# A fifth block of exponentials on VectorE in four groups of the last two quads, with a new order of all tasks

## The chip, the core and the metric

The kernel runs on one core of a Trainium2 chip. The metric is the device time of one execution in microseconds, the median of the runs. TensorE is called PE, ScalarE ACT, VectorE DVE, GpSimd POOL and SyncE SP, as in the profile.

## The reference

The input is a sequence of 2048 tokens of 640 numbers in bf16. It goes through an attention branch with 32 heads of 20 numbers each and through a mixing branch, and the two are multiplied:

```python
xn = _layernorm(x)
s = _A_ref(xn, A_wqkv, A_wo)             # softmax attention, 32 heads, then @ wo
g = _silu(_B_ref(xn, B_w1, B_w2, B_w3, B_w4))
return x + s * g

def _A_ref(x, wqkv, wo):
    ...
    scores = jnp.einsum("bhqd,bhkd->bhqk", q, k) * (Dh ** -0.5)
    p = _softmax(scores, axis=-1)
    o = jnp.einsum("bhqk,bhkd->bhqd", p, v)
    ...
def _B_ref(x, w1, w2, w3, w4):
    h = _gelu(_layernorm(x) @ w1)
    ...                                  # four column groups of h, each shifted along the sequence by 1 or 2
    x1 = x + hs @ w2
    return x1 + _gelu(_layernorm(x1) @ w3) @ w4
```

The attention needs 32 x 2048 x 2048 exponentials, 134 million.

## The kernel before

**Tiling.** The 32 heads are taken in eight quads of four (0 to 7), the 2048 queries in four chunks of 512; a quad and a chunk together are a group, written (quad, chunk). Within a group the keys come in 16 tiles of 128. For one key tile the scores of four heads fill four PSUM banks of 512 columns. Two heads (a pair of banks, 1024 columns) are computed by one step on PE: either as two matmuls over 32 rows of the array each (row form, L1596), or, where the neighbouring steps on PE are of another kind, as eight matmuls over 128 rows against queries masked by head (masked form, L1611).

**Exponentials on ACT.** `exp_act` (L1658) reads a pair of banks and writes 1024 exponentials in bf16. In a few tiles ("wide", L1640) one instruction takes all four banks. Then one set of four matmuls, one for each head, multiplies by the values and adds to bank 7 (L1409).

**Exponentials on DVE.** For some pairs of key tiles, called blocks, half of the scores go to DVE. `score_both` sends one pair of heads of a tile to ACT and the other to DVE, which multiplies the scores by a constant, adds another and writes 16-bit integers whose bits, read as bf16, are an approximate exponential (L1689). `block_bits` makes three more copies, each with a constant added to the integers (L1575 on DVE, or L1573 on POOL for those (group, block, copy) that `PP` lists), and four sets of four matmuls sum all four versions (L1587); the last two take values scaled by a constant (`VP`). Two blocks make one unit of 4096 columns; a fifth block is a unit of its own with 2048 columns. `ND` says for every group how many blocks it has, `UNITS` at which place in the row of key tiles they stand, and `BLK` which key tiles they are:

```python
self.BLK = [(2, 3), (6, 7), (10, 11), (14, 15), (0, 1)]
self.ND = ([2, 4, 4, 4],) + tuple([5, 4, 5, 4] for _ in range(6)) + ([4, 4, 4, 4],)
```

`NR` lists the places of the wide tiles (100 + place) among the tiles that are in no block. The last chunk of quad 7 is computed in two halves by other code (`last_half`).

**Repeats.** `AGAIN` names score steps, by (quad, chunk, key tile, pair), that are computed once or several times more than needed; the same result is written again.

**Ends of groups.** `normalise` transposes bank 7 (L1711, DVE), takes reciprocals, multiplies (L1724, POOL) and stores the group's result in DRAM. In quad 7 the output projection follows (L710 with 320 columns, L1823, L1842, L1885): for chunk 3 the part of the first seven quads after group (7,0), for a whole chunk after its group.

**Other work.** The B branch (w1, w2, w3, w4) and the projections for the next quads go on beside the attention, in the same queues.

**Order.** `program` makes the tasks in program order with the buffers that they read and write. A long string, `TABLE`, then gives the order of all 5722 tasks, two characters for a task and one for each PSUM bank set or buffer that it takes. `follow` decodes it, assigns the banks, and sets row or masked form by the neighbours on PE. `plan_sync` makes the semaphore waits from it. Each engine works through its own tasks in that order. A POOL task waits by semaphore for the last fast DVE task ahead of it in the table.

Of the kernel before, what the change touches and what calls it, by code (L numbers as in the profile page):

```python
# [639 lines left out]
class Gen:  # L640
# [1475 lines left out]
    r"E&p%v($C%6&q&c&d%;&r%x#',$'-$I'.%y%w$J&e$K*:#$g$h*.$%G&s$A%z$L$i'/%{%|'0&{%*;)$j$B$k&|&}&~*5#*/%'1%}#/$l'#*6&'%$'&'''(')*=$&_#5'$$m$M%~'**8#$n&:%&;%Y#*9'%J$&"
    r"<%K&=&>%T&%O'%Z%[%P%Q$o'2(K%L*>$&?(L%U*<%M%t%V%W%]%_(%`%a%b%R%^'+#0&t%X%F%H%S%I(T&#)&$%c%N&%*3'*?#&&&'&*(&+&((M*4(*@)&,&-&.&/'?%'@'A'B'C&)&L$&C#&1*0#&2&6)&M&"
    r"N&O'D&P&0&D&@&7&Q*D$*1'*E#*F#*2&E*G*R(&F*S%&G&8(*7*n#*I(&9*o'&H*M&*A'M('N*K'O*N$'P'Q*H#&A%*B*J)(N&u$&v&w'R&B*O&*C*P&'E'3(&x'4&y&z*v#*L'5'6*w('7'8*T&*X(*l#'9("
    r"*U)':*Z';'<*m#&R&I&3'=*V'>*[&*^%*](*Q*W#'F('G'H+4'I'J*Y)*_*x&+&('K*}#*y$*b&5*h'Y(*p'Z'[*k&S)'h'S#+'&'T'U']'^*s((U*~)'V'W&T'L'_*t#'X*z*{$+6#*`*q'+8(P'a$(O'`'b"
    r"'c'd*|$'e*r%'f+:$++#+,(+#*c+)'+<*e&J$*a+D#+5$*d&K+*)+F*u+W''j$'k+7'+H$+X#+Y#+Z%'l'm'n+J+9'+$#+m$'o+-+;$*j+%)'p#*g*i+M*f+(+.+n(+S+c#+e+>('q+?)+@$'r+[+G('s't+A"  # L2120
    r"&'u&m+b#+I%+g$+i+/+=+C'+d#'v$'w+E''x+f#+k$'y'z+B'|#'}+P,A+l$+0'{+U+h)+v$+p(+q&+x+o'g+V,2#,3'+T'~+r(+s%+z$+|(#($,/#+Q+O+j,-$,0$,K(,7#+N+t,.),L((%'i+K,)+~,1+L,"
    r"C$+]'.W(&#7+1(Q$,8%(',E(R+}+_#+^$+R+y$,G',I,+,*+`),4#,&+{&,5#()$(*+a,#+u',9$(+(,,6,((-,:),'+2,Q#,B$+w$(((.,$,;,T',S,,,%(/$,D#,U$&41F,l#,V%(0,F',m)(1(2,<1G(3,"
    r"H$,W,M#,N&,P$,R',X(5#,J(4(6(7,j(,Z,p#,O(8,k#(9,z$,r,d,g#(S(^(V,{&,t(,h%(:,v,n(;#(<,s$,u)(=(>,x#,y#,}((?(@,[(_((`(a(b-'#(z,e&,|,~'(c,a,^,f(-#(,Y,c-$$-+&-L-)(A"
    r"-r#-s#,i,].X(d---0,o(,`,b-%-&&,q((e-*#(W((X(Y(Z([(]-($(B-2-:&,_-,',w({(-;%-=#->)-3(H(|(}(~)#-4(D-6-B&-N(-5-<)$-C(-?#-1-9-P-@%-D(-R$(C#(E-T-Q#-/(F-A-M$#8-E$-]"
    r"(-S&-_-F-O)-7-.,=-X#-Y$-V(-a&.l(-c-8-`#.m+3,>-G.n-W(.o-b%(G-[(-w&.p-U-e-H.Y&-^'-x).Z.[.q-f-p%-{(.].^._.`#-}.a(I(J-i-q&(l.b-Z-u$.)#.c.d-t-o.f$.g-v$-~$.e.E'.h)"
    r",.i.j.*#2W(s.k)H.$%)%-y.##.F)-z$.%-|$.s-k)&$)'.''.,#)(-g.(()).-'.&.G$,?.r.6'-l-j)*.+.H%..#.8-n-h-d.1'./$.2$.I.5#.0.3(.t)+.7)(f$.M'.4.>.;-m(g(h.J$.N#(i.K$(j.u"
    r"#.v.w(k,@.x.y)3.@.O(.P'.z2Y$2b#.?.D2[.{#.<.:2h(2d$.Q2j2c).|.}2^#2e(2l(&f.A-I-J2]$.~/#2`.=2_#/$2n.L.92k#2g$.B.C2m%2i&/%#/&/'/(2}#2X(/).R.S2f2q2~$/+(/,/-/.2Z)3"
    r"&#/*3''//2r32&3*(2s33(/02t2z3,2a3)#-K(t((u3.&34(3+)(v(w30(x35#3;#37(38&(y)A3:3=%2u36)B(2o3K#39&3<&3-(3J3>)C3L#3/&2v3$#7;)D)E)F3R&2{(2w3D313k3A2p3F2y3%%)O2x3G"
    r"2|(3S)3()G.T3M(3Z#3B/13N'3#3U&)-().)/3]3W$3P(3V#3?3Q()03Y&)13X)23@3l(3m#3T3[%3C3o3n&44$3O3I3q(4v3w#3e3_3H45)3s3u&3x'3v%3E3c3a3`(m(42#3{(3^(n)V3}3p&3d3b43#3f3"
    r"r$(o3z#4#(4%4@&3y/4(p(q3|(.U.V4B%46/23~#(r4(4$#47(4')I#)J)K)L48))M4J$49#)N413g3t/3$4:'4K$):/5/64&)P#)l)Q4E#4=(4<$)R)S)T4;4.4+3h4F#4>(4?4G#4H&4A(4*4S$)U4U))4#"  # L2130
    r"4D4I4P#4C4R4O(4Q#4k$4l&)5)6)74L(4T#4V4M%)84c4i$4)4,4-4d#4f(4/4j#404g(4m);()94e#)<)=4n&4o&)>)?4X4]4Y)@4_4h)^4{#)W()X)e)Y4w&4}#4y(4x(4z4Z)Z4N)[4`4^5-#5/%4|(5&&"
    r"4W4p)]*%6-4~4[4a4b5'')_(5*#)s5)()`)a5?&5+)4q)b)c5@&5G(5,5.#5#)f#)d50595I$5$$5%#5H(5=#5<)g)h5K$5>(5J5L(4r5M)5D#)i)j5N5E%)k525()m()n5P(5V#565R&5Q#5X/9)o)p)q5S'"
    r"5A5B(5Z#5O5U&)r5])t(5C&5W))u5;5j(5Y#53515l&575T5k$5m()v)w/7585c)x5o(/85q&5[#54555:)y*&'5`5n*'*(*)**5f*+5r'){&5_5p$5y$5u'5w5{*,@g@o$)|)}@p@q@r5s)~*#5^@s@u%@v)"
    r"z5i*$@w63$@t6/#65@x@{#@i$*-61@j@k3i3j@l@|@y@z@}5b@~A#A$5h6=#6?5t$1E@m1^%1_1V#1`1W1X1Y1Z1[1a1b1k&1l1O'5g5v#1H#1m1n1c@n1o6%1I1J1K1L1M1P5a1Q1p1R1S1T6@(5}/G#/H6B"
    r"'/I6A$6.#4s/J/K60)5x(5z$6C4t4u5d5e67$69#6:(/L1e#1f1g1h1i6#6'1]5F1j5~6F68#62(6P#6Q$6$/;#/</=/>/?/@64%@h6I6&6L5|6<$6>&6(6[#/S#6^/T/U/V6;7S6d(6e#6`$6b6f#666E6R("
    r"6H6g(/W/:/X<(6Z$6o#6q6)6O6J/`#/a6S%6])6U(/b/c6V'/d6k$6s#6l&6G6T6r(/e/A#/B6u6x/C/D6t$/E6n#/F6W$6K6p%6h/M$7=/N6w6M6X#/O/P6_#7&'6D6{/Q6Y/R7</f(7?7%7@7A/g7'(6i&7"
    r"((6N6~/h/i/j/k6a$6z6c6j#6|A&6}6y70$/Y#7))/Z/[/]7*71$6m7-(7.#/^/_6v7F7+#7879<*$/x#=;/y<,7,)/z/{/|7><)(<+&6*7#<.$<4#<5'7$/}7//l#72<2(<0<3)<8$<7#/m/n/o73/p<:<6<"
    r"-(/q<<$<9#<R#</)0(#0)<>0*0+0,0-<S$<M(<K$<A<@04#<N%<?0506<Z#<]<;(07<C0809<L'<1<U$<B<=(<W&<P#<Q)<V(<J0L#7C0M0N0O0P<d$<O<f#<i#<X6+0Q<Y(0X#0Y0Z0[0]7E<D<[%<a$<F<k"
    r"<E<_#<b'0^<e(7B19#1:<T<h$1;1<1=<G7G<`(7D<j)<g<^=##<x(<m<H<z$<I1>0e#<n<y$<{%<w0f<q0g0h0i=$)<p='$7:7H=&(=(#0j<l=)0q#0r0s0t0u0v<}#<t=+$=-=*(<|<~&=,$0}#0~1#F-1$1"
    r"%1&0@'0A0B0C0D74=A$0E=@(=C=51-#1.1/1011<u12=E#=B%==(=?=_$<o<s=F#/r#=%=`$<r6,<c=G#75=/=H)A%=<(=>&<v>H/s/t76/u=1/v=.=2=3=K#/w=J$=0=M=4=67I=L'7J7M/~#=N(0#=P(7O0"  # L2140
    r"$0%0&0'=f#=I=O$7K=a(=g)0:#=Q0;0<=^0=0>0?=i#0.(=b#8V0/000102=703=j(=l=d&=c=k'=t#0F(0G0H=e(=u#0I0J0K=n&=p77=m(=o$=h=Z0R(8L0S0T0U0V0W=r#=s)=}(=w&=D13(14>#151617"
    r"18>%#=x%=8=y(=v>$$>'=T=z&>&#1'#1(1)1*=S7b>6#=|(=~)1+1,>7(={0_(0`0a8S0b0c=q=V>9&>:$>@(>A'=90d0k(0l0m1?&0n8P0o=W1@1A0p1B1C1D0w#0x=:=U>>$>*7Q>?%>4#>5&>J(0y0z0{7"
    r"P>3=R=Y>n$>o)>L=X=[>q#=]>r#>8>;$>](>B>,>->/>M#>(>_8W><&>N$>s(>+>P>O%>)>=>l#>t'>X$7L>m$>[(>^&>.>0>20|>1>R#>S(>Z>CA'>b>W$8Q7R>T(7N7T#>u>p7U7V>Y'>w#>y>d>I$7W7X7"
    r"Y>c>U)>K#>k>V>v#>z(>x&>|(>{$A.#A/A0A1>e>h8M>}A2>QA3?J#?L)?-$>`?/?#(7Z?$%7[#7]7^8N?)#?+?($7_7`?*$7a?%(>f?&#>~?A$?,#?.'>gA(#>a?[A)?2A*>j>i?F#?G(7p?B&?H(?5A+?'?"
    r"<$A,?I?=#?7?4A-?;?K#?a(?>$?8?c$A4#A5?M??%A6A7A8>D?C(AJA9?D'?b#?3?1A:(?0?U?f&?o(?O?q)?d?g(?6?:A;?E?Q?9A<?^#7i?](?_&A=?@?k&?S?`A>A??R?m#?p(?r?h#?P?N?i%>E?T7c#?"
    r"V7d@*$@+'@##>F?l(?n7e7f?~7g7h@$)?j@%$@&#?u7j$7k@.#@-'@/%7l?e@'@($@0@2'@6#7m@47n@)&7o@1$@7)@C'@3#@8#@,7q$@E7r@?$@>'?x?z@A7s@9$7t7u@:@;$@@&8T7w7x#@F8X7v?v?w@<'"
    r"8R@B(@D$@5@G7y@]#@_$?y7z@^)?s@`#?{?|@=8O?tAL(8UFnA@Fr@W#?}AC7{@H@J@K@X%@R$7|@S'@M8Y@a@Y#AAANAP(7}@L@T$@N7~ARAB#ADAE@Z(@[A_#Aa@U)AV(AW#F.A^$8##8$8)8%AZ(AT#@P>"
    r"G@V8Z80?W?X@IA`%A|$AU(AY#A]AdA~)8[8_AO(@QAQ$8&8'8(@O@b8*(8cA[&B^8+8,8-Ay&An(Ao'8.8/AbAmAK#AM%Ap(AX81(82Aq&83A{A}#Au&84Av#ASFt@cB#8586As(B/&AgB%#B1FuAt$Ar87Af"
    r"B&%AhAwAi8>?YBH(Bh$B+#8?#8@8A8B8CBJ&B-AeB.(8EBi#Ax#B0$Aj8DB4B7Az'Ac88(898:8;B'&BC(BD(AkAlB:8<8=B$B3B6BI#B()B*(B,'BKB28F(8G?ZB)FxBL&BN)BM#BE(8H8I8JBF%BOB=B@&B"
    r"n#8KBpC%(BWB58aB;BA'C&)B>&BQB`#B8C'(B?&B<8]B9BBBbBm&Bj#C($Br(Bo&BUBSBGBk%BPBRB_&8`BVBtBa(BT8e@dBd#Bq(Bs'Bc&BXC)BlC/(8d8b8^Bf8lCiC*#Be)8f(8g8h8i8j8zC1$BgC0(Bw"  # L2150
    r"BzC+#8kC;&C$8m(C3#C28n8o8p8q8rC<%C5'B}C8&C9(CE#BuBv9%8{(8|8}CGC7C,#C-$8sCD&CF&C4(8~9#C:B{B|C@#CB)C6CA(9$CCByCV&Bx@e@fB~CW'CSCMC_#C`(C=(8t(8uCJC>)C#C.8vCHCa&C"
# [81 lines left out]
```

## Time and profile before

| | |
|---|---|
| time, three runs | 795.1, 794.38, 794.72 us; median 794.72 |
| profiled execution | 794.99 us; span 793.2 us, clock 0.998 |
| ACT | busy 765.9 us, 97% of the span |
| PE | busy 773.7 us, 98% (modelled ends of matmuls) |
| DVE | busy 688.2 us, 87% |
| POOL | busy 441.5 us, 56% |
| exponentials on ACT | 726 of 1024 columns, 13 of 2048 |
| reads of scores on DVE (L1689) | 268 |

The profile is one execution. The busy time of a group of instructions counts overlapping instructions once, so that count times mean can be more than it. "Idle before" is the time that an engine stood still ahead of an instruction of the group, with what ended it behind the arrow. Windows give times from the start of the span.

### The profile page before, as it was taken

How to read it: one execution, taken by the hardware profiler on the slowest of the kernel's cores; microseconds unless marked ns; L12 is line 12 of the kernel's file. 1: busy time of each engine (PE TensorE's matmuls, PEld its weight loads, DVE VectorE, ACT ScalarE, POOL GpSimd, SP SyncE). 2: the span in 40 equal slices, each digit the busy share in tenths (PEclk: the TensorE clock that was granted, in tenths of full speed). 3: DMA queues.
4: the chain of work that ended last, by engine and by line, in shares of the span. 5: the costliest groups of instructions: out<-in, count | busy, mean ns of one | idle time of the engine just before them, and what ended most of it. 6: DMA issues, size and time to landing. Idle time of an engine off the chain costs nothing.

```text
span 793.2 us, 29655 instructions
## 1 busy us (share of the span) xinstructions
PE 773.7 (98%) x13432; PEld 321.6 (41%) x13432; DVE 688.2 (87%) x914; ACT 765.9 (97%) x798; POOL 441.5 (56%) x238
## 2 busy tenths in 40 slices
...
GB/s 176 70 74 60 97 135 65 78 119 37 38 87 35 55 66 56 72 76 68 79 95 52 26 83 53 86 36 94 53 93 45 36 42 82 26 20 133 104 142 94
DMA packets 141357, 58.22 MB, mean 73 GB/s; under 512 B 113728, under 2 KB 136432, under 8 KB 141232
## 3 DMA queue, kind: packets, MB, share of 16 engines
...
q8 instruction: 105, 1.72, 0.9%
q14 instruction: 20, 0.16, 0.1%
...
## 4 chain that ended last, share of the span: by engine, by line
ACT 56%; PE 37%; DVE 4%; DMA 1%; issue 0%; SPq 0%; DVEq 0%
ACT arena L1658 49%; PE psum L710 14%; PE psum L1596 8%; PE psum L1587 5%; PE psum L1409 4%; PE psum L1611 3%; ACT arena L2069 3%; DVE arena L1689 2%; ACT arena L1640 2%; ACT arena L1977 1%; ACT arena L2097 1%; PE psum L1466 1%; DMA arena<-arena 1%; PE psum L1440 1%; ACT L1658 0%; DVE arena L921 0%
## 5 line engine op out<-in xcount | busy, mean ns | idle before, releaser
L1658 ACT ACTIVATE arena<-psum 128x1024 bf16<-128x1024 f32 x726 | 678.3, 1038 | 14.3 <-PE psum L1596 11.0
L1573 POOL TENSOR_TENSOR arena<-arena 128x2048 int32<-128x2048 int32 x92 | 330.2, 3599 | 224.8 <-DVE arena L1575 104.7
L1689 DVE TENSOR_SCALAR arena<-psum 128x1024 uint16<-128x1024 f32 x268 | 326.3, 1219 | 54.8 <-PE psum L1596 49.2
L710 PE MATMUL psum<-arena 128*32 128x320 bf16 (+1 forms) x5808 | 336.0, 332 | 1.0 <-DMA arena<-in_B_w_dram 0.4
L1596 PE MATMUL psum<-arena 32*128 32x512 bf16 x1646 | 197.0, 384 | 9.1 <-ACT arena L1658 5.7
L710 PEld LDWEIGHTS psum<-arena 128*32 128x32 bf16 x5808 | 142.9, 96 | 120.9 <-issue 30.8
L1587 PE MATMUL psum<-arena 128*22 128x512 bf16 x2144 | 186.9, 380 | 0.0
L1409 PE MATMUL psum<-arena 128*22 128x512 bf16 x1448 | 136.7, 381 | 0.3
L1575 DVE TENSOR_SCALAR arena<-arena 128x4096 uint16<-128x4096 uint16 (+1 forms) x127 | 133.2, 1072 | 2.5 <-PE psum L1587 1.8
L1596 PEld LDWEIGHTS psum<-arena 32*128 32x128 bf16 x1646 | 54.4, 91 | 176.9 <-ACT arena L1658 97.4
L1611 PE MATMUL psum<-arena 128*32 128x512 bf16 x1512 | 114.9, 381 | 0.3
L1587 PEld LDWEIGHTS psum<-arena 128*22 128x22 bf16 x2144 | 52.4, 91 | 61.2 <-issue 25.6
L1724 POOL TENSOR_TENSOR arena<-arena 128x512 bf16<-128x512 f32 x30 | 40.8, 1362 | 27.3 <-DVE arena L1575 20.0
L1409 PEld LDWEIGHTS psum<-arena 128*22 128x22 bf16 x1448 | 35.6, 91 | 47.2 <-issue 21.7
L1611 PEld LDWEIGHTS psum<-arena 128*32 128x32 bf16 x1512 | 31.7, 95 | 40.8 <-ACT arena L1658 30.1
L2062 DVE CAST arena<-psum 128x512 bf16<-128x512 f32 x48 | 32.7, 682 | 4.5 <-PE psum L710 4.3
L1276 DVE CAST arena<-psum 128x512 bf16<-128x512 f32 x40 | 27.3, 687 | 8.0 <-PE psum L710 7.8
L1885 POOL TENSOR_TENSOR arena<-arena 128x640 bf16<-128x640 bf16 x12 | 16.7, 1401 | 21.1 <-DVE arena L1823 6.5
L1640 ACT ACTIVATE arena<-psum 128x2048 bf16<-128x2048 f32 x13 | 24.7, 1898 | 0.7 <-PE psum L1596 0.7
L921 DVE BATCH_NORM_STATS2 arena<-arena 128x6 f32<-128x320 bf16 x54 | 24.9, 482 | 0.4 <-DMA arena<-in_A_x_dram 0.3
L1823 DVE SCALAR_TENSOR_TENSOR arena<-psum,arena 128x320 bf16<-128x320 f32 x32 | 15.4, 486 | 9.7 <-PE psum L710 9.7
L1711 DVE STREAM_TRANSPOSE arena<-psum 128x512 f32<-128x512 f32 x30 | 21.3, 711 | 1.9 <-PE psum L1587 1.3
...
## 6 DMA issues: line engine op xcount, KB each, us to landing
...
heads<-arena SPq DMA_DIRECT2D x120, 20.0 KB, 2.0
...
```

What stands on the lines that cost most here:

```text
L710: ins = e.matmul(pb[32 * c:32 * c + 32, 0:N], lhsT(k, c), rhs(k, c), start=(k == 0), stop=(stop and k == nk - 1), tile_position=(0, 32 * c))
L1409: ins = e.matmul(pb[32 * i:32 * i + 22, 0:512], VA[:, ql, kts[i // 2], i, :], PT[:, slots[i // 2][0].slot, 512 * (i % 2):512 * (i % 2) + 512],
L1573: return e.tensor_tensor(dst.bitcast(I32), U[:, ub, 0:w].bitcast(I32), bass.AP(c.tensor, c.offset, [list(c.ap[0]), [0, w // 2]]), op=ALU.add)
L1575: fa if onp else lambda e, v=v, dst=dst: e.tensor_scalar(dst, U[:, ub, 0:w], EXP_B[v], None, op0=ALU.add),
L1587: ins = e.matmul(pb[32 * i:32 * i + 22, 0:512], wv, dst[:, at:at + 512].bitcast(BF16), start=first, stop=final, tile_position=(0, 32 * i))
L1596: return e.matmul(out, self.KT[32 * i:32 * i + 32, b, 128 * kt:128 * kt + 128], q, start=True, stop=True, tile_position=(32 * i, 0))
L1611: ins = e.matmul(out[32 * c:32 * c + 32, :], self.KT[:, b, 128 * kt + 32 * c:128 * kt + 32 * c + 32], self.QM[:, gb, 2 * a + jj, :], start ...
L1640: lambda e: e.activation(self.PT[:, hp[0].slot:hp[0].slot + 2, :], self.psum[:, 512 * h0.slot:512 * h0.slot + 2048].rearrange("p (a b) -> ...
L1658: lambda e: e.activation(self.PT[:, hp.slot, :], self.psum[:, 512 * hs.slot:512 * hs.slot + 1024], AF.Exp, scale=cfg.scale),
L1689: ins = e.tensor_scalar(U[:, ub, 1024 * at + 512 * k:1024 * at + 512 * k + w], self.psum[:, 512 * hd.slots[k]:512 * hd.slots[k] + w], a_ex ...
L1724: return e.tensor_tensor(OnT.rearrange("p (k d a) -> p a k d", k=4, a=4), Ob[:, :].rearrange("p (a k d) -> p a k d", a=4, k=4), in1, op=AL ...
L2062: T("dve", c_dve(512), lambda e, h=h, fc=fc, i=i, G=G: e.tensor_copy(G[:, i, fc, :], self.wbank(h)[:, 0:512]), reads=[wa], writes=at, name ...
```

## The change

Groups (6,1), (6,3), (7,0) and (7,1) have five blocks instead of four, so that key tiles 0 and 1 of these groups become a block as in the other groups with five. (6,1), (7,0) and (7,1) keep one wide tile each, at place 5, 4 and 5 among six tiles outside blocks instead of place 6, 6 and 5 among eight; the entry that goes from (6,3) named a place that did not exist there. The list of repeats is another one, with 10 repeats in place of 20. `TABLE` is replaced as a whole: another order and other banks for all tasks. Instructions keep their forms, and no function is changed. Code behind these lines stands five lines lower than before.

```diff
@@ class Cfg, __init__ @@
         self.ND = ([2, 4, 4, 4],) + tuple([5, 4, 5, 4] for _ in range(6)) + ([4, 4, 4, 4],)
-        self.NR = tuple(tuple(tuple(x for x in g if x >= 100) for g in q) for q in self.NR)
+        self.NR = [[tuple(x for x in g if x >= 100) for g in q] for q in self.NR]
+        self.NR[6][1] = (105,)
+        self.NR[6][3] = ()
+        self.NR[7][0] = (104,)
+        self.NR[7][1] = (105,)
...
-        self.AGAIN = {(2, 2, 5, 0): 1, (2, 2, 7, 1): 1, (2, 3, 4, 0): 1, (3, 1, 7, 1): 1, (6, 1, 3, 0): 1, (6, 1, 6, 1): 1, (7, 1, 0, 0): 3, (7, 1, 0, 1): 1, (7, 1, 2, 0): 3, (7, 1, 5, 0): 1, (7, 1, 5, 1): 1, (7, 1, 6, 0): 1, (7, 1, 10, 0): 2, (7, 1, 15, 0): 2}
+        self.AGAIN = {(7, 0, 8, 1): 1, (7, 1, 1, 0): 1, (7, 1, 4, 0): 1, (7, 1, 5, 0): 1, (7, 1, 6, 0): 1, (7, 1, 7, 0): 1, (7, 1, 7, 1): 1, (7, 1, 9, 0): 1, (7, 1, 11, 0): 1, (7, 2, 15, 0): 1}
         self.EARLY = 4
+        self.ND = ([2, 4, 4, 4],) + tuple([5, 4, 5, 4] for _ in range(5)) + ([5, 5, 5, 5], [5, 5, 4, 4])
...
 TABLE = (
-    r"#6#9#p#:%r#_$O#%#&$P#;#<$N&V#`#a#b#c#g###=#>#?#@#A#B#C#D#E#F#G#H#,#f#(#-#)#d#I#J$+#'#$#*#+#2%s#.#4#k#j#l$W#i#t#K#L#m#r$X$Y#e#n#q$Q$R#o$S$T#u#s#v#w$U$V#}#M$#%"
...
```

More of the change, by code (lines that the diff above doesn't have):

```diff
@@ L2116 @@
[L2116 to L2127, printed above, removed]
@@ new lines @@
+    r"'#O#P%(#$U#~$%#z#Q#R#S#T#U$&$X$Y$Z$V#y#V#W#X$z)${$|#e$}%)%*%+#Y$v%#$$]$[$~%,$/$+$,$'%$%%$-$q%&$^#Z$w$x#[$r$s$*#h#f$_&U$y$e%'$t$0$`#]#^#d%k)%d(%e&X#$a$b&Y&Z&["
+    r"%l%m%f%2$$c%g%7'%n$(%h$E$)%r%<&%3$f&]$.%-%%8%4%o%5%i%9%=%.%/%>%6$H$1$=$2$3$G%0&g(&h%?&i%1%@$C#0&`$%:&j&a&b&c&d$<%A%%B$9$6$7$:%p%C%D%;&n&$>&o$;%u%j$?$4$I&^%v#"
+    r"$D&e&k$F$@%w%E$5$J&p&q&r$A&s&{$%x%&l$g%q%y&|%z%{&}&~'#*.#*:&%|'%('&'''($h'$#/$K$B$i$j',$*;%%G$M$k')'-$l*/''*'.$L$m*8&'/$n&:($o*5#&m'0*9#&;&<*6)*=&&=&>%O'%P*>"
+    r"('1%Y&%Z%Q%F%T$%U%[*<%}%V%R%W%]%_#%H%I(K(T%`%a(L%~&?%S%J(%s%K%L%M%b%c%X%^%N&#)&$&@(M&%*?#*3'&&&'&(*4#%t*@&&*$&+&,&-&.'?#'@'A'B&/&1&2&3&0'C'D*0#*1$&L%&M&6(&N&"
@@ new lines @@
+    r")&7&O&P&Q&C#&D*D#&_'+*E$*G(N*F%*R(*2&E&F&G*S$&8&&9*7*n%*I(&H*M&*o)*A'M&'N'O'P'Q*K*H%&u$&v&w&x&y*B'R*N#*O&'3&&A%&B*J&*v%&z'4'5*P(*L*w''6'7'8*T&*U%*l(*m&*X%*Z'"
+    r"9&':*Q&t*C'E';'<'='>*[&*^#*]%*W('F&'G'h'H*p'2#5*_'I*x&*Y(&5*y)'J'K*}%+&(*V*b'Y&'Z'S)'T'U'[']'V'W+'&'^&R&I*s(*~$&S#*t%'X'_*k*{$+4+6#*z&T*q(*|#+8'a#'b'c'd'e+:$"
+    r"'f++#*d*c+<*r)+)'&J$+,'*u+5#&K+*(+D$*`+F+#+W',A'j$+-+7)+Y#+H$+X#'k+Z''l+9''m'n+$#+;(+J+m$*a+%%'o*e*h'L(P*i*g*f'p#*j+n$+>(+M+c#+(+.'q'r+@$'s+e+?%+[+G(+A&'t'u+"
+    r"=+g#+I#+b$+d)+S+i+/+B+C'+E%'v$'w+k$+f#'x'y+l&'z+h((O'|#'{'}'~+V+v$+p((#+x+q#($,2#,3'+U+o+N+z(+r$+j+0+s$,/#+K,0)+T(%+P+Q+|,-&,K(,7#+t+O'g'i,.&,L('`(U+R&4(&#7,"
@@ new lines @@
+    r")+~+}+L,8#,1+]'(',C$+_#,E(Q$+^)(R+y$+`&,G',I+{$,+,*,#,4#+a()$,9$+u'(*(+,5%(,,6,&,:),%,$,B#+w%,Q$,;,S(-,D#,',T'(.,V),(,U$,l#,,(/$(S(V1F,W(0,F',m&(1(2,H$,M$+1,"
+    r"P#(3(z,R%,<(^+2,X,J(5#(6(7(8,p#-L(4,j((9,N$.W,r,d,z$,Y,k',O,g(,{),t#,h((:,n(;#,v,s$(<(=(>,x#,}(,u%(?,y#(_(,~'(`,a,c,Z,](@,e#-'&-)(a,[-#((b(e,=(A,^(c,f&(I,|-+"
+    r"#-$$-r&(d,i--,o(-s),q&-0(W((X,`-&&(l-*#(Y(Z([,_+3-((-,#-%(]-3(B,w-:&-;$({((|(s)%(}(~(D)#,b-=#-/-9-N()$((-P-B&->&(C((E-?#-C'(F-@#-1-<#8-D(-E$-R&-..l(.m-2-Q#-]"
+    r"(-T-S%-M&-F-_(G-6-O$.n.o,>-7.p-X#-a(-V&.q-A-8.X-4-c-5-G-f-Y(-W#-`#.Y$.Z-w$-b&-['.[.].^-Z-U-{#-^'-p'-x$-q%._-o.`$-}-i-H(J.a.b.c-u$.)#(H.d.f#-l1G.g.h.i.e.j.k-v"
@@ new lines @@
+    r"#.*(-~(.E$.F'-y,?-d-t-z#)&#-k)'.$$-g.'$-|).#()(-j.(&)).,#.s)*.&.-%.%.6(&f.G$.H$-n.+)+..#.8(f#(g-h,@.2$./).4.1(-I.3#.;(h.I.5#.0-m.7'.r.M(.N$(i(j.J$-e.D.9(k.>."
+    r"u$.v.w2W.x.y.O'.z.K%2Y#.=.{$.|.P(2b$.t2h'2[.}.~.A2d#2c'2j/#.:-J2e)/$2^$2]'.Q.L.?2`.@.<2_#2l#2n)3),2k()H2g$2m$.C.B2i&/%#/&/'.R/(2}#2X(/)2~%2f2q.S2t/+(/,-K/-/*"
+    r"/.3&#//2Z()O/03')2z3*(32&2s3,2a3)#33$(t((u3+&(v2w34&3.((w35#(x3;#2r2o30/13=(37&39'38(2u(y3:2v363K#3<$3>3-')B$)C3J3L#3/$3$#2y)D2{'3R$31)E3%')F)A3@2|(3(3S$2x2p"
+    r"3k3M#3Z'3D3A3N&)G3E3?3U$3W))-$).)/3P#3]3V'3X3G.T3O3Y$3Q'3[#)04v.U)13F)23l#3n&3m'3^3T44$3o3a45$3H3e3w#3x#3q'3B3C3s3u$3b3#3I42#3{(3_3c3v)(m#3`3p$3}43%3r'3d(n(o"
```

144 lines of the change are left out of this document (71 added, 73 removed).

## The prediction

> **What bounds the kernel now.** I read the page's busy table and chain first, then the busy time by window, then the chain of waits in order of time, then groups of instructions by line in single stretches.
>
> ```profile
> span 793.2 us, 29655 instructions
> ...
> PE 773.7 (98%) x13432; PEld 321.6 (41%) x13432; DVE 688.2 (87%) x914; ACT 765.9 (97%) x798; POOL 441.5 (56%) x238
> ...
> ACT 56%; PE 37%; DVE 4%; DMA 1%; issue 0%; SPq 0%; DVEq 0%
> ```
>
> ACT is busy for 765.9 of 793.2 us, and 56% of the chain that ended last is ACT. PE's 98% is a modelled figure and has to be checked by its waits. The totals hide the stages, so here are the stretches that matter (columns: stretch, its length, busy time and instruction count of PE, weight loads, DVE, ACT, POOL, then clock, DMA share, GB/s).
>
> ```profile
> 40.00:600.00 560.00, 554.30 (x9142) 217.88 (x9134) 501.75 (x619) 550.25 (x561) 321.33 (x146) 1.00 0.32 70
> 220.00:340.00 120.00, 118.46 (x1922) 46.93 (x1914) 114.39 (x155) 115.25 (x122) 70.29 (x32) 1.00 0.30 61
> 540.00:600.00 60.00, 59.28 (x992) 23.10 (x984) 51.46 (x57) 59.97 (x61) 30.95 (x11) 1.00 0.31 70
> 600.00:740.00 140.00, 135.48 (x2364) 56.65 (x2360) 114.07 (x127) 139.36 (x143) 73.00 (x28) 1.00 0.27 59
> 740.00:786.00 46.00, 45.66 (x1090) 26.65 (x1092) 35.08 (x59) 43.06 (x45) 25.04 (x14) 1.00 0.41 118
> ```
>
> Where are the four changed groups? Each group but the first ends in one transpose of L1711, and those of quad 6 and the first two of quad 7 stand here in the timeline:
>
> ```profile
> 624.24 0.71 DVE L1711 STREAM_TRANSPOSE arena<-psum 128x512 f32<-128x512 f32 x1
> 646.05 0.71 DVE L1711 STREAM_TRANSPOSE arena<-psum 128x512 f32<-128x512 f32 x1
> 667.76 0.72 DVE L1711 STREAM_TRANSPOSE arena<-psum 128x512 f32<-128x512 f32 x1
> 689.79 0.71 DVE L1711 STREAM_TRANSPOSE arena<-psum 128x512 f32<-128x512 f32 x1
> 708.41 0.72 DVE L1711 STREAM_TRANSPOSE arena<-psum 128x512 f32<-128x512 f32 x1
> 739.18 0.72 DVE L1711 STREAM_TRANSPOSE arena<-psum 128x512 f32<-128x512 f32 x1 [0.16 <-PE psum L1587]
> ```
>
> So (6,1) runs to 646, (6,3) from 668 to 690, (7,0) to 708, (7,1) to 739: all four lie in 600 to 740, where ACT idles 0.64 us in 140 and DVE idles 25.9. The chain in order of time says the same (start, length, what):
>
> ```profile
> 640.66 42.29 ACT arena L1658 x46
> ...
> 755.83 1.36 PE psum L710 x40
> ```
>
> Forty-six exponentials follow each other without a gap, then after 740 the chain is PE work of the output projection. What the change takes from ACT before 740 can therefore move the end; the tail of 46 us behind it is bound by PE and can only move as a whole.
>
> **What goes from ACT.** A fifth block turns two key tiles from four exponentials on ACT into two on ACT and two on DVE. Four groups, so 8 exponentials less; the wide ones (L1640) stay at one each in (6,1), (7,0) and (7,1). An exponential's mean of 1038 ns overlaps its follower, so its price is the pitch of the chain: 42.29 / 46 = 0.919 us. 8 x 0.919 = 7.35 us off the path. With this alone the stretch would take 132.65 us instead of 140.
>
> **What DVE gets.** Per block two reads of scores (L1689) and three shifted copies of 2048 (L1575), because the fifth block is in none of the lists that send a copy to POOL. The first row is from the groups in 600 to 740, the second from the page-wide groups by form, the third and fourth from the timeline of (6,2), a group that has five blocks already:
>
> ```profile
> L1689 DVE TENSOR_SCALAR arena<-psum 128x1024 uint16<-128x1024 f32 x51 | 62.2, 1221 | 16.9 <-PE psum L1596 16.3
> L1575 DVE TENSOR_SCALAR arena<-arena 128x2048 uint16<-128x2048 uint16 x36 | 23.5, 687 | 0.4 <-PE psum L1587 0.3
> 663.16 1.36 POOL L1724 TENSOR_TENSOR arena<-arena 128x512 bf16<-128x512 f32 x1
> 664.79 1.89 DVE L1575 TENSOR_SCALAR arena<-arena 128x2048 uint16<-128x2048 uint16 x3
> ```
>
> 2 x 1.22 + 3 x 23.5/36 = 2.44 + 1.96 = 4.40 us a block, 17.6 us in four. DVE would then have 114.07 + 17.6 = 131.7 us of work in 132.65: 99.3%. No stretch shows DVE that full. The nearest row is 220 to 340, at 114.39 / 120 = 95.3%, and there ACT is not saturated any more. Its idle time before exponentials, first in 220 to 340 (both forms), then in 600 to 740:
>
> ```profile
> L1658 ACT ACTIVATE arena<-psum 128x1024 bf16<-128x1024 f32 x121 | 113.9, 1026 | 4.2 <-PE psum L1596 3.2 <-PE psum L1409 0.6
> L1640 ACT ACTIVATE arena<-psum 128x2048 bf16<-128x2048 f32 x1 | 1.9, 1877 | 0.5 <-PE psum L1596 0.5
> L1658 ACT ACTIVATE arena<-psum 128x1024 bf16<-128x1024 f32 x132 | 122.9, 1047 | 0.6 <-PE psum L1596 0.4
> ```
>
> When DVE is late, PSUM banks stay taken, PE's next scores (L1596) come late, and ACT waits for these: 3.2 + 0.5 = 3.7 us in 120. Over 132.65 us that is 4.1, against 0.4 now: 3.7 us lost. To be at 95.3% at all, DVE may hold 0.953 x 132.65 = 126.4 us there, so 5.3 us must move out. The whole order is new, and neighbours have room: 540 to 600 can take 0.953 x 60 - 51.46 = 5.7, and 740 to 786 has 10.9 idle. So I take the loss of 3.7; its ends are 0 (all hidden, as in 600 to 740 today) and 5.5, where nothing moves out and DVE at 95.3% needs 131.7 / 0.953 = 138.2 us, leaving a gain of 1.8.
>
> [...]
>
> **PE.** Per block, two sums over values (L1409) become one, and four over the shifted copies (L1587) are added: three sets of four matmuls more, 12 in all.
>
> ```profile
> 644.76 0.61 PE L1587 MATMUL psum<-arena 128*22 128x512 bf16 x8
> 666.18 0.39 PE L1587 MATMUL psum<-arena 128*22 128x512 bf16 x4
> PEld psum L1596 <- ACT arena L1658: 21.4, 54, 0.7
> ```
>
> Eight take 0.61 and four 0.39, so a set costs 0.22 us: +2.6 us. Against that the table of repeated scores falls from 20 repeats to 10 (14 to 8 in (7,1)); at 0.22 (rows, one set) to 0.44 (masked, two sets) each that is -2.2 to -4.4. Net -1.8 to +0.4; I take 0. The cover is the 21.4 us in 54 waits in which PE waited for ACT in 600 to 740 (third row); without it the cost is 0.4. In the tail there is no such cover, but of all this only the repeat in (7,2) falls in it, 0.2 us. That PE can close up its work by 7.35 us in the stretch rests on the same 21.4 us.
>
> **POOL and the queues.** POOL's work is the same; no DMA is added or removed, the loads and stores only stand elsewhere in SP's order, and I cost that at nothing: the DMA share is 0.27 in the stretch. If the output's fetches came late, PE's tail would show it.
>
> **The new order elsewhere.** Decoding the old and new tables over the tasks made before (6,1), 79% of ACT's successive pairs are unchanged, 29% of PE's; row-form score pairs go from 617 to 621, masked ones from 149 to 145. ACT idles 560 - 550.25 = 9.75 us in 40 to 600. Its bounds are a gain of all of it and a loss of as much again; since a fifth of ACT's neighbours change I put 0, with 2.0 either way.
>
> **Sum.** Profiled execution: 794.99 us, a span of 793.2 and 1.79 around it; it stands 0.27 above the median of 794.72. 794.99 - 7.35 + 3.7 = 791.34, and 791.1 on the median.
>
> **Rivals.** First, all is hidden: DVE's extra work fits its idle time and ACT stays at 99.5%. For: in (6,2), with five blocks, ACT has no gap in the chain. Against: DVE's 99.3%. It gives 794.72 - 7.35 = 787.4.
>
> Second, DVE becomes the bound and nothing is won. The stretch takes 131.7 / p for a DVE occupancy p: 138.2 at 95.3% (792.9), 140 at 94.1%, 141.6 at 93% (796.3). For: the extra 17.6 us falls in the stretch that loses 7.35. Against: the room outside. About 794.7.
>
> [...]
>
> That the change doesn't do what it says is hardly possible, since groups with five blocks exist already in quads 1 to 6; it has no chance of its own.
>
> **How the numbers follow.** Chances: forecast 0.43, all hidden 0.17, DVE bound with no change 0.17, slower 0.23. The forecast's own range is 787.4 to 792.9. The range for 8 in 10 runs from 786.0 (all hidden, with most of the 2.0 of the new order) to 798.0 (the third rival's near end and part of the 2.0); what lies outside is mainly that rival's far end. A measurement of this kernel can tell about 0.2%, 1.6 us, from no change: 793.1 to 796.3. Faster 0.43 + 0.17 = 0.60, same 0.17, slower 0.23.
>
> **What would show it.** Right: L1658 (its line moves down by five) x718, L1689 x276, copies of 2048 x48, L1587 x2208, L1409 x1432; ACT busy near 758.5, DVE near 705.8, POOL unchanged; DVE near 95% and ACT near 97% from 600 to 733; the PE-bound tail of some 46 us as it was. [...]

## The result and the profile after

The changed kernel takes 792.46 us (median of 7 runs, 792.01 to 794.28) against 795.02 us (median of 7 runs, 794.25 to 795.3) before: a ratio of 0.9973, 95% interval 0.9961 to 0.9984. By the ratio that is faster by 2.2 us, 0.27%, with an interval of 1.3 to 3.1; the medians lie 2.56 apart. The forecast was 791.1 in a range of 786.0 to 798.0. The sum came out about right; most of its terms didn't.

The page of after: span, busy times, shares of the chain that ended last.

```profile
span 790.3 us, 29581 instructions
...
PE 773.1 (98%) x13382; PEld 320.8 (41%) x13382; DVE 705.3 (89%) x934; ACT 760.0 (96%) x790; POOL 441.2 (56%) x238
...
PE 62%; ACT 35%; DVE 2%; DMA 1%; issue 0%; DVEq 0%
```

The counts are those that the change announces: 8 instructions less on ACT, 20 more on DVE, the same on POOL. Busy time moved as well: ACT 765.9 to 760.0, DVE 688.2 to 705.3. The chain turned over, from 56% ACT to 62% PE, and yet the span is only 2.9 us shorter. The windows of after, with the same columns as those of before:

```profile
40.00:600.00 560.00, 554.76 (x9206) 219.35 (x9206) 509.32 (x624) 551.57 (x560) 323.39 (x147) 1.00 0.32 71
600.00:740.00 140.00, 136.56 (x2268) 55.51 (x2264) 124.20 (x142) 134.73 (x137) 68.31 (x28) 1.00 0.22 52
600.00:733.00 133.00, 129.56 (x2124) 52.12 (x2120) 117.47 (x132) 128.88 (x131) 64.19 (x25) 1.00 0.23 52
740.00:786.00 46.00, 43.72 (x1090) 25.93 (x1078) 36.90 (x64) 39.60 (x42) 24.55 (x13) 1.00 0.43 126
```

From 600 to 740 ACT now idles 140 - 134.73 = 5.27 us, where it idled 0.64. What was taken from it has become idle time there. The ends of the groups (6,0) to (7,1), the transposes of L1716, show where the time was won:

```profile
619.89 0.72 DVE L1716 STREAM_TRANSPOSE arena<-psum 128x512 f32<-128x512 f32 x1 [0.65 <-PE psum L1414]
642.29 0.71 DVE L1716 STREAM_TRANSPOSE arena<-psum 128x512 f32<-128x512 f32 x1
663.68 0.72 DVE L1716 STREAM_TRANSPOSE arena<-psum 128x512 f32<-128x512 f32 x1 [0.35 <-PE psum L1414]
685.13 0.70 DVE L1716 STREAM_TRANSPOSE arena<-psum 128x512 f32<-128x512 f32 x1
709.62 0.71 DVE L1716 STREAM_TRANSPOSE arena<-psum 128x512 f32<-128x512 f32 x1
735.20 0.72 DVE L1716 STREAM_TRANSPOSE arena<-psum 128x512 f32<-128x512 f32 x1 [0.24 <-PE psum L1592]
```

Group (6,0) ends at 619.89 instead of 624.24: 4.35 us earlier, before any changed group has ended. From there to the end of the span it is 790.3 - 619.89 = 170.41 us, against 793.2 - 624.24 = 168.96: 1.45 us longer, with 8 exponentials less on ACT. In these two executions the whole gain lies ahead of the changed groups. The lead is no accident of the two: of the kernels described below, the one that computes everything up to (6,0) as before does reaches this point at 624.72, and the five that compute it as after does at 619.62 to 621.16. (A cut at the end of a group is not quite a cut through the same work, since the order differs; behind it after has 161.0 us of PE work left and before 158.8.)

### The profile page after: what moved, and what is told of

The parts are those of the page before. It is cut to its first block, busy times and chain, and to the rows that moved or that the text cites. A ratio compares the mean times of both kernels' runs of the same rounds, so it can differ in the third digit from the quotient of the medians.

```text
span 790.3 us, 29581 instructions
## 1 busy us (share of the span) xinstructions
PE 773.1 (98%) x13382; PEld 320.8 (41%) x13382; DVE 705.3 (89%) x934; ACT 760.0 (96%) x790; POOL 441.2 (56%) x238
## 4 chain that ended last, share of the span: by engine, by line
PE 62%; ACT 35%; DVE 2%; DMA 1%; issue 0%; DVEq 0%
ACT arena L1663 30%; PE psum L715 22%; PE psum L1601 14%; PE psum L1592 10%; PE psum L1414 7%; PE psum L1616 6%; PE psum L889 1%; ACT arena L2074 1%; ACT arena L1645 1%; ACT arena L1982 1%; DVE arena L1694 1%; PE psum L1471 1%; ACT arena L2102 1%; DMA arena<-in_B_w_dram 1%; PE psum L1445 0%; PE psum L1061 0%
## 5 line engine op out<-in xcount | busy, mean ns | idle before, releaser
L1663 ACT ACTIVATE arena<-psum 128x1024 bf16<-128x1024 f32 x718 | 671.5, 1036 | 16.9 <-PE psum L1601 11.5
L1694 DVE TENSOR_SCALAR arena<-psum 128x1024 uint16<-128x1024 f32 x276 | 335.3, 1219 | 46.9 <-PE psum L1601 43.3
L1601 PE MATMUL psum<-arena 32*128 32x512 bf16 x1644 | 199.3, 384 | 7.0 <-ACT arena L1663 3.5
L1580 DVE TENSOR_SCALAR arena<-arena 128x4096 uint16<-128x4096 uint16 (+1 forms) x139 | 142.2, 1041 | 3.6 <-PE psum L1592 2.9
L1616 PE MATMUL psum<-arena 128*32 128x512 bf16 x1440 | 109.5, 380 | 0.3
L1716 DVE STREAM_TRANSPOSE arena<-psum 128x512 f32<-128x512 f32 x30 | 21.3, 710 | 2.7 <-PE psum L1592 1.6
```

The source lines that it names most:

```text
L1580: fa if onp else lambda e, v=v, dst=dst: e.tensor_scalar(dst, U[:, ub, 0:w], EXP_B[v], None, op0=ALU.add),
L1601: return e.matmul(out, self.KT[32 * i:32 * i + 32, b, 128 * kt:128 * kt + 128], q, start=True, stop=True, tile_position=(32 * i, 0))
L1616: ins = e.matmul(out[32 * c:32 * c + 32, :], self.KT[:, b, 128 * kt + 32 * c:128 * kt + 32 * c + 32], self.QM[:, gb, 2 * a + jj, :], start ...
L1663: lambda e: e.activation(self.PT[:, hp.slot, :], self.psum[:, 512 * hs.slot:512 * hs.slot + 1024], AF.Exp, scale=cfg.scale),
L1694: ins = e.tensor_scalar(U[:, ub, 1024 * at + 512 * k:1024 * at + 512 * k + w], self.psum[:, 512 * hd.slots[k]:512 * hd.slots[k] + w], a_ex ...
```

## The experiments

Each kernel ran beside the kernel before on the same chip, whose median was 794.77, 794.99 and 794.82 us on the three chips that were used. Ratios are against it; after's own is 0.9973. "Behind" is the time from the end of group (6,0) to the end of the span in the profiled execution: 168.96 us in before, 170.41 in after.

**ACT's relief alone, old order.** Made from the kernel before:

```diff
+EIGHT = {f"{quad}_{qc}_{kt}_{1 - kt}" for quad, qc in FOUR for kt in (0, 1)}
...
+        few = 64 if tag in EIGHT else 1024
...
-               lambda e: e.activation(self.PT[:, hp.slot, :], self.psum[:, 512 * hs.slot:512 * hs.slot + 1024], AF.Exp, scale=cfg.scale),
+               lambda e: e.activation(self.PT[:, hp.slot, 0:few], self.psum[:, 512 * hs.slot:512 * hs.slot + few], AF.Exp, scale=cfg.scale),
```

> The old kernel, in which the 8 exponentials on ACT that the change moves to DVE (key tiles 0 and 1, one pair each, in the four groups) compute 64 of their 1024 columns; the rest of these weights is left out. DVE and PE keep the old work. A short one costs about 0.11 us (1.028 us less 960 columns at the 0.843 ns that 1024 and 2048 columns differ by, less the overlap), so ACT has 8 x 0.81 = 6.5 us less. If ACT's pitch is the price, as the prediction has it, and PE can close up: 788.0 to 789.0. If PE cannot close up its work in the stretch, so that it takes over as the bound by itself: 791 to 793.

Measured: 794.89 us (11 runs), ratio 0.9998 (0.9989 to 1.0007). Nothing: neither range of its expectation held. Here is its chain in order of time in group (6,2), the group that in before lay inside the row of 46 exponentials without a gap (start, length, what):

```profile
641.10 14.69 ACT arena L1663 x16
655.78 0.05 issue
655.83 0.40 PE psum L1600 x4
656.23 0.33 PE psum L1591 x4
...
667.02 0.48 PE psum L1615 x8
667.50 0.64 PE psum L1591 x9
```

Behind the short exponentials ACT is ahead, and from 655.8 to the group's end at 668.2 the chain is PE work, piece after piece. The same stretch of before shows how near PE was to being the bound (window, columns as above):

```profile
655.00:667.76 12.76, 12.51 (x216) 5.16 (x214) 11.40 (x15) 12.76 (x15) 6.33 (x3) 1.00 0.47 93
```

ACT was busy all of 12.76 us and PE for 12.51 of them. A second bound lay a quarter of a microsecond under the first, as far as PE's modelled busy time can tell.

**PE's relief, without and with ACT's, old order.** Both from the kernel before; the second has the edit above too:

```diff
+                    cols = 64 if quad > 5 and not first else 512
...
-                        ins = e.matmul(pb[32 * i:32 * i + 22, 0:512], wv, dst[:, at:at + 512].bitcast(BF16),
+                        ins = e.matmul(pb[32 * i:32 * i + 22, 0:cols], wv, dst[:, at:at + cols].bitcast(BF16),
```

> The kernel before; in quads 6 and 7 the sums over values of DVE's shifted copies take 64 of 512 columns, except a group's first set, so part of the outputs is left out; some 110 sets of four matmuls at about 0.22 us become short, 10 to 15 us less work for TensorE, ScalarE's and VectorE's work as before. If TensorE sets the pace there together with the banks: 3 us or more faster, 792 or less, with the last part (198.5 us) at 195 or less. If ScalarE's chain of exponentials sets it, as the chain of waits of before says: no change, 794.3 to 795.5, since its 0.64 us idle of 140 leaves nothing to win. If the order and the waits for banks tie all three engines: also no change to 1.5 us, but with ScalarE's idle time as before and TensorE's longer.

> The same short sums in quads 6 and 7, and besides the eight exponentials that the change moves off ScalarE compute 64 of 1024 columns: both parts are left out of the outputs. Alone the short exponentials gave nothing (794.9 against 794.8). If that was because TensorE was the other bound, both together give more than the sum of each alone: another 3 to 7 us below the kernel with short sums only. If ScalarE's relief is lost in the order (banks that VectorE frees, groups that wait for each other), this kernel stands within 1 us of the one with short sums only.

Measured: 794.25 us (11 runs), ratio 0.9996 (0.9987 to 1.0005), and 794.11 us (12 runs), 0.9992 (0.9983 to 1.0). Busy time fell as meant, PE from 773.7 to 761.0 and 760.6, in the second ACT to 760.5. With some 13 us of PE work and 5 us of ACT work gone, the two together are worth about 0.7 us, 1.4 at most by the interval. The first kernel fits two of its three theories (one of them but for 0.05 us): its chain is still 55% ACT, and short sums alone can't tell a bound on ACT from a tie of all engines. The second kernel decides between its own two: it stands within 1 us of the first, so ACT's relief is lost in the order. Some of what it is lost to shows in the chain of the kernel with both reliefs, at two places:

```profile
662.57 0.41 PE psum L714 x12
662.98 0.04 PE psum L1616
663.02 6.72 DMA arena<-in_B_w_dram
669.74 0.10 issue
669.84 0.32 PE psum L714 x4
...
716.41 0.62 SPq L1752
717.03 0.04 issue
717.08 4.34 DMA heads<-arena
721.43 0.38 SPq L1809
721.81 0.04 issue
721.85 3.84 DMA arena<-heads
725.69 0.04 issue
725.74 1.54 PE psum L714 x40
```

A third layer comes up: a load of weights, which by the chain starts when PE is done with its buffer (6.72 us), and the way of the attention's outputs through DRAM (`heads`: out in 4.34 us, back in 3.84) on which the output projection waits. None of them stands in before's chain between 600 and 740. They are not all of it: from 625.4 to 767.6 transfers of these kinds are 14.6% of the chain and the exponentials of 1024 columns still 49.7%. No run shortens the transfers, so what they are worth is not shown. The two slowest of the 11 runs with PE's relief alone, 796.1 and 797.33 us, had a mean granted clock of 0.991 and 0.990, the others 0.995 to 0.998.

**The new groups' work, piece by piece, new order.** Four kernels made from after, with 64 columns instead of the full width for, in turn, the other eight exponentials of the four fifth blocks, their 16 sums, their 12 copies, and all of the work of these blocks at once (reads of scores too):

```diff
+EIGHT = {f"{quad}_{qc}_{kt}_{kt}" for quad, qc in FOUR for kt in (0, 1)}
...
+        few = 64 if blocks[0][0] == 4 and (quad, qc) in FOUR else w
...
-                  fa if onp else lambda e, v=v, dst=dst: e.tensor_scalar(dst, U[:, ub, 0:w], EXP_B[v], None, op0=ALU.add),
+                  fa if onp else lambda e, v=v, dst=dst: e.tensor_scalar(dst[:, 0:few], U[:, ub, 0:few], EXP_B[v], None, op0=ALU.add),
...
+                    few = 64 if j == 4 and (quad, qc) in FOUR else 512
```

> The changed kernel, in which the other 8 exponentials of the four new blocks, those that stayed on ACT, compute 64 of 1024 columns (the rest is left out). ACT has 6.5 us less again. If ACT still sets the pace of the stretch: 786 to 787. If PE or the banks that DVE gives back set it, as the chain with 62% PE from 600 to 740 reads: 790.5 to 792.5.

> The changed kernel, in which the 16 sets of matmuls that sum the four versions of the four new blocks take 64 of 512 columns (the rest of these sums is left out). PE has about 16 x 0.19 = 3.0 us less, more than what the change added; DVE and ACT are as before. If PE's added work is what ate the gain: 789.5 to 790.5. If it is DVE's added work, as the prediction has it: 792.0 to 792.8.

> The changed kernel, in which the 12 shifted copies of the four new blocks on DVE take 64 of 2048 columns (the rest is left out; the sums read older numbers). DVE has 12 x 0.55 = 6.6 us less, PE and ACT are as before. If DVE's load delays the scores and with them ACT, as the prediction has it, a good part of the 3.7 us lost comes back: 789.5 to 791. If PE's added work is the cause: 792.0 to 792.8.

> The changed kernel, in which all work of the four new blocks is short at once: their 8 exponentials on ACT, 8 reads and 12 copies on DVE take 64 columns, and so do the 16 sums on PE (the rest is left out; the scores stay). Each alone gave at most 0.6 us. If the order ties the engines so closely that each one's relief is used up by the next one's load: 785 to 789. If something that no engine's load shows bounds this stretch (transfers, or the tail): 791 to 792.5.

Measured: 791.91 (ratio 0.9964, 0.9952 to 0.9977), 792.79 (0.9975, 0.9966 to 0.9984), 792.63 (0.997, 0.9959 to 0.998) and 791.22 us (0.9954, 0.9942 to 0.9967). No single piece is told apart from after; all together stand 1.2 us below it by the medians, and their interval still overlaps with after's. The short sums and the short copies each came out in the range that blames the other, so neither is to blame. With everything short, the profiled execution has 789.2 - 619.88 = 169.32 us behind group (6,0): about what the old kernel needs there with its four blocks and all of its work (168.96). So in the new order too no one engine's added work sets that part. All of it together costs at most 170.41 - 169.32 = 1.1 us there, and even without it, with 16 full exponentials less on ACT than in before, the part is no shorter than the old one.

**The order ahead alone.** Two kernels made by joining the two orders: after's table up to a task, then the kernel before with its four blocks and its order for the tasks that are left. The seam lies behind 4312 tasks in the first (inside group (5,3)) and behind 4440 in the second (behind the long activations near 590 us). A third is the other way round: the old order for 4430 tasks, then after's.

```diff
-        self.AGAIN = {(2, 2, 5, 0): 1, (2, 2, 7, 1): 1, (2, 3, 4, 0): 1, (3, 1, 7, 1): 1, (6, 1, 3, 0): 1, (6, 1, 6, 1): 1, (7, 1, 0, 0): 3, (7, 1, 0, 1): 1, (7, 1, 2, 0): 3, (7, 1, 5, 0): 1, (7, 1, 5, 1): 1, (7, 1, 6, 0): 1, (7, 1, 10, 0): 2, (7, 1, 15, 0): 2}
+        self.AGAIN = {(6, 1, 3, 0): 1, (6, 1, 6, 1): 1, (7, 1, 0, 0): 3, (7, 1, 0, 1): 1, (7, 1, 2, 0): 3, (7, 1, 5, 0): 1, (7, 1, 5, 1): 1, (7, 1, 6, 0): 1, (7, 1, 10, 0): 2, (7, 1, 15, 0): 2}
...
```

> New order and banks for the first 4312 tasks (up to the first task of group (6,1)), then the old kernel: four blocks in the four groups, the old order of what is left, the old repeats there, and new banks or buffers for 5 tasks where the two parts meet. Theory A, formed from the two traces: the new order ahead of the changed groups brings all of the gain (the second pair of long activations, L2069, starts at 591.14 instead of 594.69 with the same 9868 matmuls done), and the fifth blocks bring nothing: 790.8 to 792.0, no slower than the change. Theory B, that of the prediction: the fifth blocks bring the gain and the order elsewhere nothing: 794 to 796.

> Nothing is left out of the computation. The order of after for the first 4440 tasks, up to behind the long activations near 590 us, and from there the four groups with four blocks each in the order of before, with the repeats of before there. Theory one (the gain of the change is the order ahead of the changed groups, the fifth blocks give nothing): the activations near 590 begin some 3 us earlier than in before, the last part takes its old 198.5 to 199.5 us, and the time is 791.5 to 792.5, the same as after's or a little less. Theory two (the fifth blocks or the new order behind 590 are needed): the lead is lost behind the seam as it was at the earlier seam, and the time is 794 or more. If the last part grows by over 3 us in the first group behind the seam, the seam itself costs too much and the run tells nothing.

> The other half: the old order and banks for the first 4430 tasks, with the old repeats there, then the changed kernel's order with the fifth blocks in the four groups (8 tasks get another buffer where the parts meet). Theory A: 795.0 to 796.0, since the stretch behind the long activations took 187.96 us before and 188.62 after. Theory B: 791 to 792.5.

Measured: 794.2 us (11 runs, ratio 0.9991, 0.9982 to 1.0), 793.78 us (11 runs, 0.9985, 0.9976 to 0.9994) and 805.08 us (4 runs, 1.0124, 1.0109 to 1.014). The first lies in the range of theory B, that of the prediction, and the third in neither range; but both lose time at their seams. In the third, group (6,0) ends at 633.04, 8.8 us later than in before, and the groups behind it have after's pace. In the first, the stretch with the seam, from the end of (5,2) to that of (6,0), takes 56.95 us, where before takes 55.52 and after 54.68; the long activations near 590 us start at 594.18, hardly earlier than before's 594.69 (after: 591.14). The second is the useful one. The windows up to the end of (6,0), from there to the end of (7,2), and the rest, first of before, then of the joined kernel, then of after:

```profile
0.00:624.24 624.24, 614.94 (x10372) 247.97 (x10372) 554.89 (x745) 607.71 (x633) 350.58 (x199) 1.00 0.33 72
624.24:767.54 143.30, 139.46 (x2521) 60.51 (x2516) 116.73 (x137) 140.40 (x148) 82.59 (x33) 1.00 0.30 72
767.54:793.20 25.66, 19.30 (x548) 13.09 (x544) 16.58 (x35) 17.82 (x19) 8.37 (x6) 0.95 0.32 103
```

```profile
0.00:621.89 621.89, 613.50 (x10400) 246.99 (x10400) 556.85 (x746) 606.47 (x633) 349.96 (x199) 1.00 0.33 73
621.89:765.30 143.41, 138.03 (x2464) 59.10 (x2456) 116.30 (x135) 140.50 (x148) 82.58 (x33) 1.00 0.29 71
765.30:791.00 25.70, 19.30 (x548) 13.09 (x544) 16.57 (x35) 17.81 (x19) 8.35 (x6) 0.95 0.34 110
```

```profile
0.00:619.89 619.89, 612.07 (x10358) 247.43 (x10358) 560.20 (x749) 605.53 (x632) 352.42 (x200) 1.00 0.33 72
619.89:762.55 142.66, 139.84 (x2458) 59.70 (x2451) 125.19 (x150) 135.96 (x140) 78.84 (x32) 1.00 0.29 69
762.55:790.30 27.75, 21.17 (x580) 13.64 (x576) 19.88 (x37) 18.55 (x20) 9.92 (x8) 0.97 0.38 124
```

The joined kernel repeats the old kernel's back part to a tenth of a microsecond (143.41 and 25.70 against 143.30 and 25.66) and starts it 2.35 us earlier. So the order ahead shortens the kernel with none of the fifth blocks. By all runs it gives 1.2 us (interval 0.5 to 1.9), against after's 2.2 (1.3 to 3.1); the profiled execution, at 792.74 us, is one of the faster ones. Its expectation put 791.5 to 792.5 to the one theory and 794 or more to the other, and 793.78 lies between them. This kernel pays at its seam too: its long activations start 3.38 us ahead of before's (591.31), and of that 2.35 are left at the end of (6,0), which after reaches 2.0 us sooner. Whether the rest of after's gain belongs to the fifth blocks with their order or was lost at the seam, these runs don't settle; the intervals overlap. One other thing that differs ahead can be ruled out by the traces: after lacks the four repeats of quads 2 and 3, but from the end of (2,1) to that of (3,1), which holds them, it takes 87.93 us against 88.14.

**The repeats, and the clock.** After without its ten repeats:

```diff
-        self.AGAIN = {(7, 0, 8, 1): 1, (7, 1, 1, 0): 1, (7, 1, 4, 0): 1, (7, 1, 5, 0): 1, (7, 1, 6, 0): 1, (7, 1, 7, 0): 1, (7, 1, 7, 1): 1, (7, 1, 9, 0): 1, (7, 1, 11, 0): 1, (7, 2, 15, 0): 1}
+        self.AGAIN = {}
```

> The changed kernel without its 10 repeated scores (8 of them in (7,1)), same order; the result is the same. PE has 2.2 to 4.4 us less from 690 to 765. If PE's load sets the pace there: 789 to 791. If the repeats stand where PE would wait anyway: 792.0 to 792.9.

Measured: 793.98 us (11 runs), ratio 0.9985 (0.9976 to 0.9994): less work for PE, and 1.5 us slower than after by the medians, 1.0 by the ratios, whose intervals just overlap. Neither range of its expectation held. The mean granted clock of its runs is 0.994 to 0.997, that of after's 0.996 to 0.999. The third column from the right is the granted clock; windows of this kernel:

```profile
720.00:722.00 2.00, 1.55 (x12) 0.38 (x9) 1.51 (x2) 2.00 (x3) 1.88 (x1) 1.00 1.01 248
722.00:724.00 2.00, 1.59 (x20) 0.49 (x22) 1.89 (x2) 2.00 (x3) 0.00 (x0) 0.99 0.59 169
724.00:726.00 2.00, 2.00 (x21) 0.66 (x23) 1.02 (x1) 2.00 (x2) 0.00 (x0) 0.50 0.30 60
726.00:728.00 2.00, 2.00 (x28) 0.56 (x24) 0.98 (x3) 0.33 (x2) 0.48 (x1) 0.66 0.78 273
```

PE is busy for 1.55 and 1.59 of 2 us, and in the next two windows the clock is 0.50 and 0.66. In its chain the price can be read, first in this kernel, then in after where the clock stayed at 1.00:

```profile
723.97 3.10 PE psum L1592 x28
```

```profile
719.12 0.54 PE psum L1592 x8
...
729.67 0.22 PE psum L1592 x4
```

28 matmuls take 3.10 us, 0.111 each, where after takes 0.54 / 8 = 0.068 or 0.22 / 4 = 0.055. At these they would be 1.5 to 1.9 us: 1.2 to 1.6 us lost in one stretch, about the difference between the two kernels. Group (7,1), which holds this stretch, takes 26.84 us where after takes 25.58. PE was busy, as the profile models it, for 3.14 of the 4 us ahead, more than three quarters.

A low share of busy time is not the whole cause. From 720 to 730 PE is busy for 8.98 of 10 us in this kernel, at a clock of 0.83. In the kernel with PE's relief in the old order it is busy for less, and the clock stays at 1.00:

```profile
720.00:730.00 10.00, 8.03 (x169) 3.62 (x158) 6.85 (x9) 10.00 (x11) 4.25 (x2) 1.00 0.49 154
```

In after PE is busy for 2.16 of the first 4 us and for 3.17 of the 4 from 340 on, and the clock from 0 to 12 and from 340 to 356 is 1.00. So what brings the clock down stays open here; in the profiled execution of after, with the ten repeats, it was 1.00 from 712 to 734.

**PE's relief, new order.** After with the short sums of the two kernels above:

> The kernel after; in quads 6 and 7 the sums over values of DVE's shifted copies take 64 of 512 columns, except a group's first set, so part of the outputs is left out; some 125 sets become short. If after's last part is bound by TensorE (62% of its chain): 3 to 8 us faster than after's 792.5, 784 to 789. If the order and the banks bind it: 791 to 792.5, since short exponentials, copies and sums of the four new blocks together gave only 1.2 us.

Measured: 792.72 us (12 runs, 789.15 to 795.53), ratio 0.9967 (0.9954 to 0.998), 0.2 us above the upper of its two ranges. The clock explains part of the wide spread. In its profiled execution:

```profile
690.00:700.00 10.00, 9.20 (x138) 3.00 (x126) 9.44 (x10) 9.86 (x11) 5.01 (x3) 0.78 0.01 2
700.00:710.00 10.00, 9.39 (x172) 3.94 (x168) 8.58 (x10) 9.51 (x10) 1.69 (x1) 0.88 0.26 38
710.00:720.00 10.00, 9.18 (x120) 3.00 (x118) 6.30 (x7) 9.74 (x11) 10.00 (x5) 0.97 0.33 93
720.00:730.00 10.00, 9.11 (x94) 2.40 (x94) 7.22 (x8) 8.10 (x8) 1.65 (x3) 0.51 0.59 154
```

The run whose mean clock was 0.998 took 789.15 us; the seven with 0.985 to 0.989 took 792.1 to 794.5. The clock is not all: the slowest run, 795.53, had 0.992. One run is no proof, but it suggests that PE's relief was worth some 3 us in the new order, and was paid back in clock.

## Why the prediction was right, and where it was right by chance

The number is right by luck. The sum won 3.6 us in the changed groups and nothing in the order ahead of them; the runs show a gain in the order ahead, and none that can be told in the changed groups.

**What goes from ACT: counts right, size off, effect wrong.** L1663 x718 and ACT at 760.0 us against 758.5 forecast; ACT's busy time fell by 5.9 and not 7.35, in part since the exponentials overlap less where gaps part them: count times mean is 726 x 1.038 - 678.3 = 75.3 us more than their busy time in before, and 718 x 1.036 - 671.5 = 72.3 in after. The step that failed is the one from "7.35 us off the path" to "the stretch would take 132.65 us". It took one chain's lack of gaps for the lack of a second bound. The short exponentials in the old order gave 0.0. The chains say why: behind ACT comes PE, with 12.51 of 12.76 us, and behind both the transfers at 663 and 717.

**What DVE gets: work right, loss right in size, wrong in meaning.** 705.3 us against 705.8. DVE stood at 117.47 / 133 = 88.3% from 600 to 733, not at 95%. The stretch did not shrink, and less work lies in it than the 126.4 us forecast: from 40 to 600, where the new order is ahead, DVE has 509.32 us of work against 501.75. ACT waits for scores as forecast (columns: the group, busy time and mean, idle time before it with what ended it):

```profile
L1663 ACT ACTIVATE arena<-psum 128x1024 bf16<-128x1024 f32 x127 | 120.6, 1029 | 5.3 <-PE psum L1601 3.5 <-PE psum L1414 0.6
```

ACT's idle time rose by 4.6 us, near the 3.7 of the sum. But DVE isn't what holds it: short copies changed nothing, and the idle time is what ACT's relief turns into when something else sets the pace. A "loss" subtracted from a gain that was not there happened to leave the right order of size.

**PE: net 0 in work, wrong cover, wrong sign for repeats.** PE is busy 773.1 us against 773.7, as forecast. But the 21.4 us in 54 waits were not room that can be closed up, and not waits of PE: the row is PEld's, the weight loads, which run beside the matmuls (321.6 us of them beside 773.7 us of matmuls, in a span of 793.2 us). In before, PE's own waits for these exponentials from 624.24 to 767.54 (first row), and those of the weight loads in 655 to 667.76 (second row), are:

```profile
PE psum L1596 <- ACT arena L1658: 2.6, 12, 0.3
PEld psum L1596 <- ACT arena L1658: 2.2, 5, 0.5
```

The weight loads waited 2.2 us for ACT where PE idled only 0.25. Over the whole stretch from 600 to 740 PE idled 140 - 135.48 = 4.52 us, less than the 7.35 that it was to close up. And the repeats were priced as pure cost, at 0.22 to 0.44 us each; without the ten that are left the kernel came out 1.0 to 1.5 us slower, with intervals that just overlap. What the ten removed ones did in the old order was not run.

**The tail.** Forecast at some 46 us, unchanged. From the end of (7,2) it is 27.75 us against 25.66, with 21.17 us of PE work in it against 19.30. So work moved into it, and the time that PE stands still in it is about the same, 6.58 us against 6.36.

**POOL and the queues: right.** POOL 441.2 us; the additions take 3592 to 3607 ns (first row), in before 3591 to 3621 (second row), and the copies of 2048 columns from 600 to 740 have a mean of 686 ns, as in before:

```profile
L1578 POOL TENSOR_TENSOR arena<-arena x92: 3592/3599/3607, 46.5 to 749.9; 128x2048 int32<-128x2048 int32 x92
L1573 POOL TENSOR_TENSOR arena<-arena x92: 3591/3598/3621, 46.8 to 751.9; 128x2048 int32<-128x2048 int32 x92
```

No run shows the third rival's time, which the range's upper end of 798.0 and the 0.23 for slower take in; the runs showed these durations, as long as before, and 792.46 us.

**The new order elsewhere: the step that decided.** Put at 0 with 2.0 either way; the lead is 3.55 us at the long activations near 591 and 4.35 at the end of (6,0). In the joined kernel 2.35 carry over to the old back part in the profiled execution, and 1.2 by all runs. In the profiled executions the lead lies outside those 2.0, and no step of the prediction accounts for it. Between the long activations of the second and third quarter of the kernel (near 381 and 591 us) the old order takes 211.5 to 212.5 us in the profiled executions, the new one 209.97 to 210.0 in all of its own: some two fifths of the lead come from there, in groups whose work the change does not touch. What in that order does it was not taken apart.

**The rivals.** All hidden (787.4): no, ACT idles 5.27 us. DVE as the bound (794.7): no, DVE has 12% idle there; its outcome, that nothing is won in the changed groups, is nonetheless what the profiled executions show, by their chains through PE, transfers and the order instead.
